# Gated linear attention and SoLU block on one core: third group's query transposes and scans exchanged, three small sums moved, and in two groups both state reads in one row

## The chip, the cores and the metric

One Trainium2 core. The metric is device time in microseconds (us) of the one core, the median of several runs. The profile is one profiled execution of the same program.

## The reference

An attention block with a decaying state, followed by a SoLU feed-forward block. Shapes: batch 4, 8 heads, 768 tokens, head size 48; 3072 tokens by 384 into 1024 hidden columns and back.

```python
for t in range(S):
    state = alpha[:, :, t, :, None] * state + einsum('bhd,bhe->bhde', k[:, :, t], v[:, :, t])
    y[:, :, t] = einsum('bhd,bhde->bhe', q[:, :, t], state)
x = y.transpose(0, 2, 1, 3).reshape(B * S, H * D)
h = x @ w_in
sm = exp(h - max(h)) / (sum(exp(h - max(h))) + 1e-9)
solu = h * sm
ln = (solu - mean(solu)) / sqrt(var(solu) + 1e-6) * g_ln
return ln @ w_out
```

## The kernel before, in words

The 768 tokens are cut into six groups of 128. A group holds 128 tokens of each of the four batches, so it has four chunks of 128 output rows. Each group goes through two parts, and the program is written so that the feed-forward of group g runs between the pieces of the attention of group g+1. Every engine works through its own queue in the order in which the program was written (the schedule is manual); engines wait for one another by semaphores. Nothing is reordered by a planner, so a step that is moved in the text is moved on every engine and DMA queue that it uses.

**Attention of group a**, in the order of the data:

- `load`, `load_v`: DMAs from SP's queue, into `an` (alpha), `kn`, `qn`, `vn`.
- `alpha_T`: alpha is transposed on VectorE (`firsts` L179 for 32 of a head's 48 columns, `lasts` L182 for the other 16) into `aT`; `scan_back` (L204) makes running products from the end, in three parts, into `hT`. `inverses` takes the reciprocal of the first column as the seed.
- `keys_T`, `keys`: keys are transposed on VectorE and multiplied by `hT` on GpSimd (L225).
- `scan_on(a, i)` (L204 too): the running products forward, in place in `aT`, for part i = 2 (the 16-column ends), 0 and 1 (heads 0 to 3 and 4 to 7).
- `lasts(qn, qe)`, `firsts(qn, qv)`: the queries are transposed on VectorE. `queries(i)` multiplies part i by `aT` on GpSimd (L253).
- `ends_of_decay` copies the group's whole decay into the last column of `qe` and `qv` (L240, L241). `move_lasts` and `move_firsts` are eight and four DMAs on SP's queue that lay queries and decay out in `q64` (printed as `lot` in the profile).
- `apart` writes two masked copies of `qe` beside `qv` on ScalarE (L245).
- `scores(a, half)`: 64 small matmuls on TensorE (L278), `masked(half)`: VectorE multiplies by the triangle (L289).
- `decay(a)`: GpSimd multiplies the state by the decay (L261). `read_state(half)`: 64 matmuls of the state with the moved queries (L333, tiles of 64 by 32); `read_values`: 128 matmuls of scores and values (L333, tiles of 128 by 32) into the same banks, then four copies on ScalarE into `x` (L363). `next_state`: the new keys and values are added to the state (L371, L381).

**Feed-forward of group g**: for each of eight column blocks s, `up(g, s)` is six matmuls of 512 columns (L394) into one of two `h` banks, exp on ScalarE (L408), h times exp on VectorE (L409, which frees the bank), a square on ScalarE (L412). `running` keeps two running sums over s, one on GpSimd and one on VectorE (both L427). `token_sums` (L454) turns these into sums by token: 32 matmuls, a transpose on VectorE (L467), and three small VectorE instructions (L469, L471, L473) whose result `d["s"]` only `finish` reads. `down(n, half)` is eight matmul steps (L507) for one chunk. `finish` scales a chunk (L532 to L548) and stores it.

The first group and most of the second are written out by hand (L699 to L843). From there a loop runs over g = 1 to 5 and s = 0 to 7. In it two tables, `first` for g = 1 and `usual` for the others, say which pieces of the attention of group g + 1 come ahead of `up` (head), behind it, after the running sums (middle), and after `down` (tail). So the attention of the third group, a = 2, lies in g = 1 by the table `first`, and that of the last two groups, a = 4 and a = 5, in g = 3 and g = 4 by `usual`. In `usual` the row at s = 6 has `read_state(0)` behind the running sums, then a `down`; s = 7 has `up`, `read_state(1)`, `read_values`.

In the third group the transposes of alpha and keys and the scans of parts 2 and 0 stand ahead of the loop (L842, L843):

```python
    scan_on(2, 2)
    scan_on(2, 0)
```

and in the loop the scan of part 1 stands at s = 1, the query transposes, their multiplications, the copies of the decay and the moves all at s = 2.

Of the kernel before, what the change touches and what calls it, by code (L numbers as in the profile page):

```python
# [9 lines left out]
FP = mybir.dt.float32  # L10
# [4 lines left out]
ALU = mybir.AluOpType  # L15
AX = mybir.AxisListType
P = 128
# [15 lines left out]
def fast_path(ctx, tc, q, k, v, alpha, moe_w_in, moe_w_out, moe_g_ln, out):  # L33
# [12 lines left out]
    nc = tc.nc  # L46
    B, H, S, D = q.shape
    NTOK, DM = out.shape
    DFF = moe_w_in.shape[1]
# [3 lines left out]
    NB = H + NP  # L53
# [8 lines left out]
    def pool(name, bufs, **kw):  # L62
        return ctx.enter_context(tc.tile_pool(name=name, bufs=bufs, **kw))
# [4 lines left out]
    small = pool("small", 4)  # L68
# [31 lines left out]
    qn = const.tile([P, H, TQ, D], FP, name="qn")  # L100
# [8 lines left out]
    SW = P + 1  # L109
# [7 lines left out]
    h4 = hT[:, 0 : NB * SW].rearrange("p (j s) -> p j s", s=SW)  # L117
# [3 lines left out]
    qv = const.tile([P, 2 * H, SW], FP, name="qv")  # L121
    qe = const.tile([P, NP, SW], FP, name="qe")
# [5 lines left out]
    gr = [dict() for _ in range(G)]  # L128
# [49 lines left out]
    def firsts(src, dst):  # L178
        nc.vector.transpose(out=dst.rearrange("p h (t u) -> p h u t", u=TQ), in_=src[:, :, :, 0:E0])  # L179

    def lasts(src, dst):
        nc.vector.transpose(  # L182
            out=dst.rearrange("p j (i t u) -> p u j i t", u=TQ, i=2),
            in_=src[:, :, :, E0:D].rearrange("p (j i) u d -> p u j i d", i=2),
        )
# [29 lines left out]
    def scan_on(g, i):  # L215
        part = slice(NP * i, NP * i + NP)
        scan(aT[:, part], aT[:, part], seed[:, part], False)
# [18 lines left out]
            i, c = divmod(b, 2)  # L236
            nc.sync.dma_start(out=q64[64 * i : 64 * i + E0, c], in_=qv[32 * b : 32 * b + 32, 0:H])

    def ends_of_decay():
        nc.gpsimd.tensor_copy(out=qe[:, :, P:SW], in_=h4[:, H:NB, 1:2])  # L240
        nc.gpsimd.tensor_copy(out=qv[:, 0:H, P:SW], in_=h4[:, 0:H, 1:2])  # L241

    def apart():
        for i in range(2):
# [41 lines left out]
    def masked(half, batches=range(B)):  # L286
        a = masks[half]
        for b in batches:
            nc.vector.tensor_tensor(  # L289
                out=sT[:, b, half * NP : half * NP + NP], in0=a[b], in1=mask[:, None, :].to_broadcast([P, NP, P]),  # L290
                op=ALU.mult,
            )
# [55 lines left out]
    def read_state(half):  # L348
        for four in range(8 * half, 8 * half + 8, 4):
            for c in range(2):  # L350
                for n, h, e in parts[four : four + 4]:
                    for i in range(2):
                        p = slice(64 * i, 64 * i + 64)
                        y_mm(2 * i + c, n, 64 * i, state[p, c, e(h)], q64[p, c, h, 0:P])
# [99 lines left out]
    def token_sums(g):  # L454


        d = gr[g]
        t = ps_a.tile([P, B, 2, 32], FP, tag="a3", name="rows") if g else ps_h.tile([P, B, 2, 32], FP, tag="h", name="rows")
        for b in range(B):
            for r in range(4):  # L460
                c = b * P + 32 * r
                nc.tensor.matmul(
                    t[quarter(r), b], lhsT=d["unit"][:, 0:32], rhs=d["p"][:, :, c : c + 32], start=True, stop=True,
                    tile_position=(0, 32 * r), skip_group_check=True,
                )
        tt = work.tile([P, B, 2, 32], FP, name="cols")
        nc.vector.transpose(out=tt.rearrange("p b i t -> p (b i t)"), in_=t.rearrange("p b i t -> p (b i t)"))  # L467
        s = sums[:, g * B : g * B + B]
        nc.vector.tensor_copy(out=s[:, :, 1:3], in_=tt[:, :, :, 0])  # L469
        sq = small.tile([P, B], FP, name="sq")  # L470
        nc.vector.tensor_tensor(out=sq, in0=s[:, :, 1], in1=s[:, :, 1], op=ALU.mult)  # L471
        d["s"] = small.tile([P, B], FP, name="s")
        nc.vector.scalar_tensor_tensor(  # L473
            out=d["s"], in0=sq, scalar=1e-6 * DFF, in1=s[:, :, 2], op0=ALU.mult, op1=ALU.add
        )

    def last_norm():

# [39 lines left out]
    def finish(n):  # L518
        g, b = divmod(n, B)
        d = st[n]  # L520
        s, whole = sums[:, n], d.get("held", d["o"])
        o = whole[:, 0:DM]
        t0 = b * S + g * P
        if g == G - 1:
            o_sb = work.tile([P, DM], FP, name="o_sb")
            r = gr[g]["r"][:, b : b + 1]
            nc.vector.tensor_scalar(out=o_sb[:, 0:P], in0=o[:, 0:P], scalar1=r, scalar2=None, op0=ALU.mult)  # L527
            nc.scalar.activation(out=o_sb[:, P:DM], in_=o[:, P:DM], func=AF.Copy, scale=r)  # L528
            nc.scalar.dma_start(out=out[t0 : t0 + P, :], in_=o_sb)
            d.clear()  # L530
            return
        nc.vector.tensor_copy(out=s[:, 0:1], in_=whole[:, DM : DM + 1])  # L532
        t = small.tile([P, 1], FP, name="t")
        nc.vector.scalar_tensor_tensor(
            out=t, in0=s[:, 0:1], scalar=-1.0 / DFF, in1=s[:, 0:1], op0=ALU.mult, op1=ALU.mult
        )
        nc.vector.tensor_tensor(out=s[:, 3:4], in0=t, in1=gr[g]["s"][:, b : b + 1], op=ALU.add)  # L537
        if g == 0:

            centred = work.tile([P, DM], FP, name="o_mean")  # L540
            nc.vector.scalar_tensor_tensor(
                out=centred, in0=mean_sb, scalar=s[:, 0:1], in1=o, op0=ALU.mult, op1=ALU.add
            )
            o = centred
        r = small.tile([P, 1], FP, name="r")
        nc.gpsimd.tensor_tensor(out=r, in0=s[:, 3:4], in1=mhalf, op=ALU.pow)  # L546
        o_sb = work.tile([P, DM], FP, name="o_sb")
        nc.scalar.activation(out=o_sb, in_=o, func=AF.Copy, scale=r)  # L548
        nc.sync.dma_start(out=out[t0 : t0 + P, :], in_=o_sb)
        d.clear()  # L550
# [166 lines left out]
    for i in (0, 2, 1):  # L717
        if i == 1:
# [3 lines left out]
            out=qe[:, :, 0:P] if i == 2 else qv[:, part, 0:P], in0=t[i], in1=aT[:, part, 1:SW], op=ALU.mult  # L722
# [98 lines left out]
    down(2, 1)  # L821
    scores(1, 1)
    masked(1)
    finish(0)
    finish(1)
    finish(2)
# [8 lines left out]
    for i in range(3):  # L835
# [3 lines left out]
    keys(2)  # L839
    load(k, kn, 3)  # L840
    down(3, 1, (2, 3))
    scan_on(2, 2)  # L842
    scan_on(2, 0)  # L843

    usual = dict(
        head={4: "keys_back", 5: "masked0", 6: "masked1"},
        behind={0: "v keys", 1: "on2 on0 on1", 2: "lasts firsts", 3: "apart", 5: "decay", 6: "alpha", 7: "back"},
        middle={6: "begin read0", 7: "read1 values"},  # L850
        tail={4: "scores0", 5: "scores1", 7: "kv"},
    )
    first = dict(
        head={3: "keys_back"},
        behind={
            0: "v", 1: "on1", 2: "lasts firsts", 3: "apart", 4: "scores0 masked0", 5: "scores1 masked1 decay",
            7: "alpha back",
        },
        tail={6: "begin read0"},
        middle={7: "read1 values over"},  # L860
    )

    def attend(a, what):

        more = a + 1 < G
        if what == "v":
            load_v(a)
        elif what == "keys":
            keys_T(a)
            keys(a)  # L870
            if more:
                load(k, kn, a + 1)
        elif what[:2] == "on":
            if what == "on2":
                inverses(a)
            scan_on(a, int(what[2]))
        elif what == "lasts":
            lasts(qn, qe[:, :, 0:P])
            ends_of_decay()
            queries(2)  # L880
            move_lasts()
        elif what == "firsts":
            firsts(qn, qv[:, 0:H, 0:P])
            queries(0)
            queries(1)
            move_firsts()
            if more:
                load(q, qn, a + 1)
        elif what == "apart":
            apart()  # L890
        elif what == "decay":
            decay(a)
        elif what == "keys_back":
            if more:
                keys_back(a)
        elif what[:6] == "scores":
            scores(a, int(what[6]))
        elif what[:6] == "masked":
            masked(int(what[6]))
        elif what == "alpha" and more:  # L900
            alpha_T(a + 1)
            if a > 2:
                attend(a, "over")
        elif what == "over" and more:
            alpha_over(a + 1)
            if a + 2 < G:
                load(alpha, an, a + 2)
        elif what == "back" and more:
            for i in range(3):
                scan_back(a + 1, i)  # L910
        elif what == "begin":
            read_begin()
        elif what[:4] == "read":
            read_state(int(what[4]))
        elif what == "values":
            read_values(a)
        elif what == "kv" and more and a != 4:
            next_state(a)
# [59 lines left out]
    def compare(out, x, bound, op):  # L978
# [6 lines left out]
        out=chunks[:, :, 2], in0=sums[:, :, 2], scalar=0.25, in1=sums[:, :, 3], op0=ALU.mult, op1=ALU.is_le  # L985
# [6 lines left out]
    else:  # L992
# [9 lines left out]
        out=bad, in0=all_ok[0:1, 0:1], scalar1=float(P * ends[-1]), scalar2=None, op0=ALU.is_lt  # L1002
# [451 lines left out]
```

## Time and profile before

| what | value |
|---|---|
| median of 3 runs | 368.37 us (367.83 to 369.05) |
| profiled execution, its time | 367.97 us |
| profiled execution, its span | 366.2 us |
| TensorE busy | 357.8 us (98% of the span) |
| VectorE busy | 245.0 us (67%) |
| ScalarE busy | 146.4 us (40%) |
| GpSimd busy | 132.2 us (36%) |
| DMA moved | 36.06 MB, mean 98 GB/s |
| TensorE clock granted | 1.0 throughout |

The span is from the first to the last instruction of the program; 1.8 us of the execution's time lie around it. Lines of the timeline give the start in us from the start of the span, the length, the engine, the line of the kernel, the operation, the tiles (output, arrow, inputs), the shape of the tile of the array for TensorE, the count, and in square brackets an idle stretch of the engine ahead of it with what ended it. Matmuls overlap in the pipe; so the distance between the starts of two neighbouring lines is what the first of them costs TensorE, not its length.

### The profile page before, as it was taken

The page shows a single profiled execution, that of the slowest core. Times are in us where ns is not written, and L with a number is a line of the kernel's source. Part 1 is how long each engine was busy: PE and PEld are TensorE (multiplying, and loading weights), DVE is VectorE, ACT ScalarE, POOL GpSimd, SP SyncE. Part 2 cuts the span into 40 slices and gives each one's busy share as a digit, 9 for nine tenths or more (in the row PEclk, how much of TensorE's full clock was granted, in tenths as well). Part 3 has the DMA queues.
Part 4 walks back from the last instruction along what each step waited for, and adds up shares of the span by engine and source line. Part 5 has one row for each costly group of instructions (what it writes and reads, how often), then busy time and mean ns, then how long its engine had stood idle before and what let it go on. Part 6 is the DMA issues. An engine that isn't in the chain of part 4 may idle for free. (4 is left out here: it accounts for less than half of the span.)

```text
span 366.2 us, 10036 instructions
## 1 busy us (share of the span) xinstructions
PE 357.8 (98%) x4341; PEld 215.0 (59%) x4341; DVE 245.0 (67%) x375; ACT 146.4 (40%) x260; POOL 132.2 (36%) x129
## 2 busy tenths in 40 slices
PE   8899999999999999999999999999999999999994
PEld 8784355666755566566575456475556565555552
DVE  0999989979998797936675935766946314345420
ACT  3647878182645262252521252431241132222110
POOL 7020000004449963774133764232773121233300
PEclk9999999999999999999999999999999999999999
DMA  9995995326196409463035354004041000000011
GB/s 180 183 338 152 204 309 124 88 67 159 50 234 141 109 21 180 85 152 94 21 92 112 83 121 126 3 25 88 21 107 55 0 25 0 24 21 22 23 47 51
DMA packets 72871, 36.06 MB, mean 98 GB/s; under 512 B 48232, under 2 KB 70000, under 8 KB 72816
## 3 DMA queue, kind: packets, MB, share of 16 engines
q1 hardware_dynamic: 71792, 34.39, 39.8%
q10 hardware_dynamic: 1024, 0.92, 0.8%
q8 instruction: 36, 0.59, 0.7%
q14 instruction: 19, 0.16, 0.2%
HBM read 25.30 MB, written 4.72 MB: 82 GB/s over the span
## 5 line engine op out<-in xcount | busy, mean ns | idle before, releaser
L507 PE MATMUL o<-w_out,room 128*128 128x385 f32 x384 | 134.0, 492 | 0.0
L394 PE MATMUL h<-x,w_in 128*128 128x512 f32 x288 | 131.7, 597 | 0.5 <-DVE g_col L642 0.5
L507 PEld LDWEIGHTS o<-w_out,room 128*128 128x128 f32 x384 | 71.0, 189 | 54.7 <-issue 13.1
L394 PEld LDWEIGHTS h<-x,w_in 128*128 128x128 f32 x288 | 53.2, 189 | 58.6 <-issue 48.5
L409 DVE TENSOR_TENSOR room<-h,e 128x512 f32<-128x512 f32 x40 | 27.5, 689 | 72.9 <-ACT e L408 72.9
L408 ACT ACTIVATE e<-h 128x512 f32<-128x512 f32 x40 | 24.0, 599 | 100.2 <-PE h L394 100.2
L427 POOL TENSOR_TENSOR p<-p,e 128x512 f32<-128x512 f32 x30 | 43.7, 1458 | 20.0 <-ACT e L408 19.9
L412 ACT ACTIVATE u<-room 128x512 f32<-128x512 f32 x40 | 25.2, 630 | 38.3 <-DVE room L409 38.3
L546 POOL TENSOR_TENSOR r<-sums,mhalf 128x1 f32<-128x1 f32 x20 | 14.8, 741 | 69.7 <-DVE sums L537 69.4
L289 DVE TENSOR_TENSOR sT<-a,mask 128x512 f32<-128x512 f32 x43 | 26.7, 681 | 8.0 <-PE a L278 7.9
L204 DVE TENSOR_TENSOR_SCAN hT<-aT,unit 128x516 f32<-128x516 f32 x18 | 24.4, 1399 | 7.6 <-ACT aT L703 7.5
L204 DVE TENSOR_TENSOR_SCAN aT<-aT,seed 128x516 f32<-128x516 f32 x18 | 27.4, 1551 | 0.2
L225 POOL TENSOR_TENSOR kT<-kT,hT 128x1024 f32<-128x1024 f32 (+1 forms) x8 | 14.2, 1800 | 32.7 <-DVE kT L179 32.7
L427 DVE TENSOR_TENSOR p<-p,u 128x512 f32<-128x512 f32 x30 | 22.5, 749 | 5.1 <-ACT u L412 5.1
L278 PEld LDWEIGHTS a<-qv,kT 32*128 32x128 f32 x704 | 21.4, 186 | 7.0 <-issue 2.6
L278 PE MATMUL a<-qv,kT 32*128 32x128 f32 x704 | 23.9, 278 | 0.4 <-POOL qv L253 0.3
L212 POOL COPY fend<-hT 128x12 f32<-128x12 f32 x6 | 3.1, 509 | 55.9 <-DVE hT L204 55.9
L333 PE MATMUL y<-sT,vn 128*32 128x128 f32 x768 | 22.6, 273 | 0.2 <-DVE sT L289 0.2
L333 PEld LDWEIGHTS y<-sT,vn 128*32 128x32 f32 x768 | 20.7, 110 | 1.6 <-issue 1.0
L196 ACT ACTIVATE sq<-an,mone 128x1536 uint8<-128x1536 f32 x12 | 18.9, 1572 | 0.2
L548 ACT ACTIVATE o_sb<-o,r 128x384 f32<-128x384 f32 x16 | 9.3, 582 | 18.5 <-POOL r L546 18.5
L261 POOL TENSOR_TENSOR state<-state,lot 128x384 f32<-128x384 f32 x10 | 8.8, 903 | 13.1 <-DMA lot<-qv 13.1
(148 smaller groups left out, 374.3 us busy)
## 6 DMA issues: line engine op xcount, KB each, us to landing
vn<-in_v_dram SPq DMA_DIRECT2D x24, 192.0 KB, 4.7
an<-in_alpha_dram SPq DMA_DIRECT2D x20, 192.0 KB, 4.1
out_dram<-o_sb SPq DMA_DIRECT2D x20, 192.0 KB, 1.9
room<-in_moe_w_out_dram SPq DMA_DIRECT2D x8, 384.0 KB, 5.5
kn<-in_k_dram SPq DMA_DIRECT2D x16, 192.0 KB, 5.6
qn<-in_q_dram SPq DMA_DIRECT2D x16, 192.0 KB, 4.1
lot<-qe SPq DMA_DIRECT2D x40, 64.5 KB, 2.1
lot<-qv SPq DMA_DIRECT2D x20, 129.0 KB, 2.4
```

Of the source, the lines that this page charges most:

```text
L196: nc.scalar.activation(out=sq, in_=x, func=AF.Relu, scale=sign, bias=mone, accum_out=over[:, g, i : i + 1])
L204: nc.vector.tensor_tensor_scan(out=o, data0=a, data1=s, initial=1.0, op0=ALU.mult, op1=ALU.add)
L278: nc.tensor.matmul(a[b][:, i], lhsT=kT[quarter(b), kb], rhs=qv[quarter(b), qb, 0:P], start=not last and not i, stop=bool(last), tile_posit ...
L289: nc.vector.tensor_tensor(out=sT[:, b, half * NP : half * NP + NP], in0=a[b], in1=mask[:, None, :].to_broadcast([P, NP, P]), op=ALU.mult,)
L333: nc.tensor.matmul(y_bank(b)[quarter(r), a], lhsT=lhsT, rhs=rhs, start=(b, r) not in begun, stop=stop, tile_position=(row, 32 * r), skip_g ...
L394: nc.tensor.matmul(h, lhsT=w_in[:, a, f * P : (f + 1) * P], rhs=d["x"][:, a].rearrange("p b t -> p (b t)"), start=(a == 0), stop=(a == KC ...
L408: nc.scalar.activation(out=e, in_=h, func=AF.Exp)
L409: nc.vector.tensor_tensor(out=u, in0=h, in1=e, op=ALU.mult)
L412: nc.scalar.activation(out=u2, in_=u, func=AF.Square)
L427: eng.tensor_tensor(out=p, in0=d[0][i] if f == 1 else p, in1=d[f][i], op=ALU.add)
L507: nc.tensor.matmul(d["o"][:, 0 : DM + 1], lhsT=u_of(g, f)[:, b * P : b * P + P], rhs=w_out[:, f], start=(f == 0), stop=(f == FC - 1), skip ...
L546: nc.gpsimd.tensor_tensor(out=r, in0=s[:, 3:4], in1=mhalf, op=ALU.pow)
```

## The change

It has three parts, which share no instruction.

1. **Third group (a = 2).** The transposes of the queries (`lasts` and `firsts`, both on VectorE) go ahead of the loop, in the place of the scans of parts 2 and 0. The scan of part 2 goes to s = 0, behind `up` and `load_v`. At s = 1 come the scan of part 0, the copies of the decay (now on ScalarE, not GpSimd), the multiplication of part 2 and the eight moves of `qe`. At s = 2 come the scan of part 1, the multiplications of parts 0 and 1, the four moves of `qv` and the load of the next queries.
2. **First group's sums by token.** The three small VectorE instructions at the end of `token_sums(0)` are put off from behind the transpose (some 25 us before `finish(0)`) to just ahead of `finish(0)`, behind `masked(1)`.
3. **Last two groups (a = 4, 5).** `read_state(0)` leaves s = 6 and stands at s = 7, just ahead of `read_state(1)` and `read_values`. For a = 2 and 3 it stays.

```diff
-    def ends_of_decay():
-        nc.gpsimd.tensor_copy(out=qe[:, :, P:SW], in_=h4[:, H:NB, 1:2])
-        nc.gpsimd.tensor_copy(out=qv[:, 0:H, P:SW], in_=h4[:, 0:H, 1:2])
+    def ends_of_decay(copy=nc.gpsimd.tensor_copy):
+        copy(out=qe[:, :, P:SW], in_=h4[:, H:NB, 1:2])
+        copy(out=qv[:, 0:H, P:SW], in_=h4[:, 0:H, 1:2])
...
         s = sums[:, g * B : g * B + B]
-        nc.vector.tensor_copy(out=s[:, :, 1:3], in_=tt[:, :, :, 0])
-        sq = small.tile([P, B], FP, name="sq")
...
+        def rest():
+            nc.vector.tensor_copy(out=s[:, :, 1:3], in_=tt[:, :, :, 0])
+            sq = small.tile([P, B], FP, name="sq")
...
+        if g:
+            rest()
+        else:
+            d["rest"] = rest
...
     masked(1)
+    gr[0]["rest"]()
     finish(0)
...
     down(3, 1, (2, 3))
-    scan_on(2, 2)
-    scan_on(2, 0)
+    lasts(qn, qe[:, :, 0:P])
+    firsts(qn, qv[:, 0:H, 0:P])
...
     usual = dict(
...
-        middle={6: "begin read0", 7: "read1 values"},
+        middle={6: "begin", 7: "read1 values"},
...
     first = dict(
...
-            0: "v", 1: "on1", 2: "lasts firsts", 3: "apart", 4: "scores0 masked0", 5: "scores1 masked1 decay",
+            0: "v on2", 1: "on0 lasts", 2: "on1 firsts", 3: "apart", 4: "scores0 masked0", 5: "scores1 masked1 decay",
...
-        tail={6: "begin read0"},
+        tail={6: "begin"},
...
-            if what == "on2":
+            if what == "on2" and a > 2:
                 inverses(a)
             scan_on(a, int(what[2]))
         elif what == "lasts":
-            lasts(qn, qe[:, :, 0:P])
-            ends_of_decay()
+            if a > 2:
+                lasts(qn, qe[:, :, 0:P])
+            ends_of_decay(nc.gpsimd.tensor_copy if a > 2 else nc.scalar.copy)
             queries(2)
             move_lasts()
         elif what == "firsts":
-            firsts(qn, qv[:, 0:H, 0:P])
+            if a > 2:
+                firsts(qn, qv[:, 0:H, 0:P])
             queries(0)
             queries(1)
...
         elif what == "begin":
             read_begin()
-        elif what[:4] == "read":
-            read_state(int(what[4]))
+            if a < 4:
+                read_state(0)
+        elif what == "read1":
+            if a > 3:
+                read_state(0)
+            read_state(1)
```

More of the change, by code (lines that the diff above doesn't have):

```diff
@@ L468, in token_sums @@
         s = sums[:, g * B : g * B + B]
-        nc.vector.tensor_copy(out=s[:, :, 1:3], in_=tt[:, :, :, 0])
-        sq = small.tile([P, B], FP, name="sq")
[L471 to L475, printed above, removed]
+        def rest():
+            nc.vector.tensor_copy(out=s[:, :, 1:3], in_=tt[:, :, :, 0])
+            sq = small.tile([P, B], FP, name="sq")
+            nc.vector.tensor_tensor(out=sq, in0=s[:, :, 1], in1=s[:, :, 1], op=ALU.mult)
+            d["s"] = small.tile([P, B], FP, name="s")
+            nc.vector.scalar_tensor_tensor(
+                out=d["s"], in0=sq, scalar=1e-6 * DFF, in1=s[:, :, 2], op0=ALU.mult, op1=ALU.add
+            )
+        if g:
+            rest()
+        else:
+            d["rest"] = rest
     def last_norm():
```

## Prediction

> **What bounds the kernel now.** I read the page's busy row first, then TensorE's timeline from end to end, then the waits of its weight loads.
>
> ```profile
> PE 357.8 (98%) x4341; PEld 215.0 (59%) x4341; DVE 245.0 (67%) x375; ACT 146.4 (40%) x260; POOL 132.2 (36%) x129
> PE   8899999999999999999999999999999999999994
> ```
>
> TensorE has work in hand nearly always, but matmul ends are modelled, so a busy TensorE may still be late. I therefore take the distance between starts. In the sixth group, where its attention lies in the loop's g = 4, the timeline has:
>
> ```profile
> 263.09 2.74 PE L394 MATMUL h<-x,w_in 128*128 128x512 f32 x6
> 265.66 2.76 PE L507 MATMUL o<-w_out,room 128*128 128x385 f32 x8
> 268.25 2.74 PE L394 MATMUL h<-x,w_in 128*128 128x512 f32 x6
> ...
> 280.88 2.07 PE L278 MATMUL a<-qv,kT 32*128 32x128 f32 x64
> 282.87 2.84 PE L394 MATMUL h<-x,w_in 128*128 128x512 f32 x6
> 285.64 1.16 PE L333 MATMUL y<-lot,state 64*32 64x128 f32 x64
> 286.74 2.86 PE L507 MATMUL o<-w_out,room 128*128 128x385 f32 x8
> 289.44 2.74 PE L394 MATMUL h<-x,w_in 128*128 128x512 f32 x6
> 292.10 1.16 PE L333 MATMUL y<-lot,state 64*32 64x128 f32 x64
> 293.19 3.70 PE L333 MATMUL y<-sT,vn 128*32 128x128 f32 x128
> ```
>
> Between whole-array neighbours an `h` row costs 2.57 us (265.66 - 263.09) and an `o` row 2.59. Next to a row of small tiles each pays 0.09 to 0.11 us a side: `h` after scores and before the state 2.77, `o` after the state 2.70, `h` before the state 2.66. From 131 to 361 us I find these same distances row for row: TensorE never waits there, and time falls only if its own rows get cheaper. Before that I find stops at three scores rows; the views show what ended the first two:
>
> ```profile
> 77.87 2.69 PE L278 MATMUL a<-qv,kT 32*128 32x128 f32 x64
> 113.12 2.26 PE L278 MATMUL a<-qv,kT 32*128 32x128 f32 x64 [0.26 <-POOL qv L253]
> PEld a L278 <- DVE qv L811: 0.3, 1, 0.3
> ```
>
> A scores row costs 2.00 when nothing is late. The second group's first one goes on to 80.49, 2.62: **0.62 late**, until VectorE's L811 (77.76, 0.69) ends. The third group's first one starts 0.32 late (12 `h` matmuls take 5.57, not 5.25), until `queries(0)` on GpSimd is done at 113.08, and takes 2.19: another 0.19, until `apart` on ScalarE ends at 114.62. **0.51 late** in all. Its second one, 2.14, waits 0.14 for a bank that `masked(0)` frees.
>
> **What the Trainium skill says.** TensorEngine Tiling (Array Packing), Key Properties: changing the tiling mode drains TensorE. The trace agrees: those 0.09 to 0.11 us a side. SBUF — State Buffer, "SBUF: two separate sides": VectorE, with two SBUF inputs, and GpSimd take a shared port pair as an exclusive lock for a whole instruction; the other blocks. The trace agrees: a scan takes 1.23 alone (the median of all), and the two at 97.56, beside GpSimd's key multiplication, 4.69 together, the longer of them 2.61; `ends_of_decay`'s copy takes 0.20 alone (72.00) and 1.13 beside a scan (106.34). A transpose has one input, and is not held: 1.11 and 2.05 beside GpSimd.
>
> ```profile
> 97.56 4.69 DVE L204 TENSOR_TENSOR_SCAN aT<-aT,seed 128x516 f32<-128x516 f32 x2
> 105.68 1.79 DVE L204 TENSOR_TENSOR_SCAN aT<-aT,seed 128x516 f32<-128x516 f32 x1
> 108.59 1.11 DVE L182 STREAM_TRANSPOSE qe<-qn 128x512 f32<-128x512 f32 x1
> 109.55 2.05 DVE L179 STREAM_TRANSPOSE qv<-qn 128x1024 f32<-128x1024 f32 x1
> 112.02 0.69 DVE L409 TENSOR_TENSOR room<-h,e 128x512 f32<-128x512 f32 x1
> ```
>
> **First sums later.** The three instructions start at 63.16, 63.37 and 63.57 and the next starts at 63.65; without them it would start as the transpose before them ends, 63.13. That is 0.52 to 0.58, I take 0.55. VectorE is then busy without a gap to L811, so L811 ends at 77.90, and the scores' stop shrinks from 0.62 to 0.07: **gain 0.55**. `apart`, the other input, ended at 77.37, and comes forward with its scan. The 0.55 comes back on VectorE after `masked(1)`: VectorE stood idle 1.97 us ahead of `masked(0)`, and with scores 0.55 earlier that idle shrinks by as much, so `finish(0)` starts at 88.0 to 88.1 as now. Behind `rest` wait only the finishes (GpSimd's power, ScalarE's outputs at 89.51 to 92.8) and the scans from 90.95; the copies of `x` at 92.95 are 0.1 us behind the last output, so the first `up`, now at 96.83, can be 0.55 earlier too. If that cover were gone, `up` would lose what is gained, no more.
>
> **Third group.** VectorE does the same instructions in another order; I walk its queue on today's clock. Keys' transposes end at 97.56. `lasts` and `firsts` cost 0.97 and 1.9 from start to start: 100.4 (today the two scans last to 102.2, held by the key multiplications; those now run unhindered, done near 100.3 instead of 101.2). L409 for s = 0: 101.0. `finish(3)`, 1.0: 102.0. Two state sums, 1.0: 103.0. Scan 2 at 1.23: 104.2. L409 for s = 1: 104.8. Scan 0, held 0.5 by `queries(2)` (1.09, from 104.2): 106.5. Running sum: 107.1. L409 for s = 2: 107.7. Scan 1, held 0.7 by GpSimd's running sum: 109.6. Running sum, held 1.1 by `queries(0)`: 111.3. L409 for s = 3: 111.9, against 112.7 today. So `queries(0)` is done near 110.7 instead of 113.08, and `apart` near 113.8 instead of 114.62. TensorE, 0.55 early and not stopped, reaches these scores at 112.25; the half that needs `apart` begins at 113.25, first with its even heads (first ScalarE instruction, near 113.15), then odd ones at 113.75. They end near 114.3 instead of 115.32: 0.55 is kept and **0.51 more gained**. The 0.14 of the second scores I leave.
>
> The other queues: GpSimd loses 1.85 us of copies (1.13 + 0.72). ScalarE gets two copies of 4 and 8 elements; no such row exists, the nearest is its accumulator read, 0.19. Two of those, 0.4 near 105.9, lie between a square and the exp of s = 2, whose VectorE partner is due only at 107.1: nothing, or up to 0.4 if that exp sets L409. SP sends `vn` (five us, behind `finish(3)`'s store, from 105.05), then the eight moves of `qe` (5.17), the four of `qv` (3.81), the queries' load. `qe` is ready near 106, so the moves follow `vn` at once, at 110.0 or earlier instead of 110.90, and `decay` (121.42 now) gains 0.9 to 1.8. TensorE reads the state at 123.00, 0.73 after the state's first half is released, so 1.06 us earlier still fits.
>
> **Both reads in one row.** With `h` and `o` side by side at s = 6, `h` loses its side (2.77 to the 2.68 of the `h` row at 275.51) and `o` its side (2.70 to 2.59). In the read row itself, matmuls come in eights every 0.109 us, the first gap is 0.14 and the last matmul is followed after 0.199; one row of 128 has these ends once: 2.06 instead of 2.18. 0.09 + 0.11 + 0.12 = 0.32 a group, **0.64 for two**. The bounds are 0.2 (the two sides) and 0.4 a group. `x` is copied at the same distance from the next `up`, with an `o` row between.
>
> **Sum.** 0.55 + 0.51 + 0.64 = 1.70. From the profiled execution, 367.97 (span 366.2 and 1.8 around it), that gives 366.27. This execution is 0.40 under the median of 368.37, so on the median's scale 366.67; I say **366.7**. A measurement of this kernel can tell about 0.3%, 1.1 us, from no change: 367.27 is the line.
>
> **Rivals.**
>
> - *The stop only moves* (0.20). TensorE comes 0.55 early, but `apart` stays tied to L409 of s = 3 and ends at 114.6 as now; both early gains are then waited away at the same place, and 0.64 is left: 367.7, within 0.3%. For it: `apart` is in ScalarE's queue behind that chain, and my walk has it only 0.8 earlier. Against: VectorE had 4.7 us of scans held by GpSimd that are now transposes, which are not held.
> - *The lock decides* (0.13), slower. In the loop each scan stands beside a GpSimd instruction. At the longest price for all three scans, 2.61 against 1.23, 1.73 and 1.9 in my walk, VectorE loses 1.4 + 0.9 + 0.7 = 3.0, and a running sum at 1.50 (today's worst) 0.7 more: L409 of s = 3 ends at 115.6, `apart` at 117.5, the scores near 118.2 instead of 115.32. 2.9 lost, 0.64 gained: 370.6. It turns slower by 0.3% once that L409 ends past 114.45, 2.5 us after my walk. For it: `scan aT` takes 2.2 in each later group. Against: that is one in three, the others take 1.21 to 1.23.
> - *The row of reads saves nothing beyond its sides* (0.05): gain 1.46, 366.9; if not even those, 1.06, 367.3 and on the line. The tiling page says that drains come with a mode change, and the modes are the same in the row, which speaks against the latter.
>
> **How the numbers follow.** The forecast gets 0.62. Its ends: 1.2 (the drop to 0.2 a group, 0.3 of the third group's stop left) and 2.3 (0.4 a group, the 0.14 and leftover 0.07 too, the later 0.05 of a state read), so 366.1 to 367.2. Adding the stop that moves and the foot of the slower case, I give 365.9 to 368.5. Faster 0.66, within 0.3% 0.21, slower 0.13.
>
> **What would show it.** Right: the second group's first scores row costs 2.05 to 2.1; the third group's 2.0 to 2.1 with no wait for GpSimd; L409 of s = 3 ends near 111 on the new clock; in g = 3 and 4 one state row of 128 at about 2.06 with `h` and `o` at 2.6 to 2.7 ahead. Wrong: scans above 2 us one after another between 102 and 110; `apart` ending at the same distance after the key transposes as now; or a new idle stretch of TensorE past 131 us.

## The result and the profile after

| | before | changed |
|---|---|---|
| median of 12 runs | 368.49 us (367.83 to 369.05) | 367.47 us (366.66 to 368.38) |
| ratio of the runs | | 0.997, 95% interval 0.996 to 0.998 |
| profiled execution, span | 366.2 us | 366.6 us |
| TensorE busy | 357.8 us | 358.0 us |

The changed kernel is 1.02 us faster (0.28%), where 1.7 was forecast. The time lies inside the stated range, beyond the likeliest case's own range, and just short of the line that divides "faster" from "within 0.3%".

The profiled execution of the changed kernel is, at 368.38, the slowest of its twelve, and its span is longer than that of before. This is why spans are not compared here. The stretch ahead of the first state matmul (`kv`, L371) is the same program in both and took 32.31 instead of 31.13 us. Most of this comes from one wait in the first group's values, which cost 5.86 us instead of 4.23 (0.6 of it is made good before `kv`, where TensorE waits less for VectorE):

```profile
23.09 0.64 PE L333 MATMUL y<-sT,vn 128*32 128x128 f32 x14 [0.20 <-DVE sT L289]
25.15 3.04 PE L333 MATMUL y<-sT,vn 128*32 128x128 f32 x102 [1.41 <-issue]
```

Behind 26 of the 128 matmuls TensorE stands for 1.41 us, and "issue" says that it waited for nothing which the profile shows: no semaphore, no DMA of the program. The experiments come back to this wait. All sums below are therefore counted from that matmul, to the lone small matmul `all_ok` near the end (L999, or L1012 in the changed kernel): 322.04 us before, 321.05 after, **0.99 less**. That this is so close to the 1.02 of the medians is partly luck: a second profile of the kernel before, taken later (`before_again`), has 322.75 there, so the difference of two single profiles is uncertain by some 0.7. Subtract 1.18 from a time after to set it beside one before.

The timeline of TensorE after, in the second group, then the third, then where the fifth group's reads lie. The line numbers behind the small sums are six higher: `down` is L513.

```profile
79.06 2.07 PE L278 MATMUL a<-qv,kT 32*128 32x128 f32 x64
81.05 2.86 PE L513 MATMUL o<-w_out,room 128*128 128x385 f32 x8
...
92.33 3.92 PE L333 MATMUL y<-sT,vn 128*32 128x128 f32 x128
96.18 1.24 PE L513 MATMUL o<-w_out,room 128*128 128x385 f32 x3
...
113.56 2.43 PE L278 MATMUL a<-qv,kT 32*128 32x128 f32 x64
115.92 2.84 PE L394 MATMUL h<-x,w_in 128*128 128x512 f32 x6
...
123.60 1.35 PE L333 MATMUL y<-lot,state 64*32 64x128 f32 x64
124.88 2.84 PE L394 MATMUL h<-x,w_in 128*128 128x512 f32 x6
...
234.82 2.74 PE L394 MATMUL h<-x,w_in 128*128 128x512 f32 x6
237.49 2.04 PE L333 MATMUL y<-lot,state 64*32 64x128 f32 x128
239.46 3.70 PE L333 MATMUL y<-sT,vn 128*32 128x128 f32 x128
```

Read the distances between starts again. The second group's first scores cost 1.99 (81.05 - 79.06), with no stop. Its values cost 3.85, where 3.63 was the price in every group but the first. The third group's first scores begin without a wait but cost 2.36, and its state row costs 1.28 instead of 1.09. The merged read row costs 1.97. Row by row, in us:

| row | before | after | difference |
|---|---|---|---|
| second group, first scores | 2.62 | 2.00 | -0.62 |
| second group, values | 3.63 | 3.85 | +0.22 |
| third group, wait ahead of the first scores | 0.32 | 0.00 | -0.32 |
| third group, first scores | 2.19 | 2.36 | +0.17 |
| third group, first state row | 1.09 | 1.28 | +0.19 |
| fifth and sixth group, reads with their neighbours | | | -0.41 each |
| sixth group, values | 3.63 | 3.87 | +0.24 |

The sum is -0.94; the 0.05 to the measured 0.99 is spread over other rows. The two long values rows, +0.46 together, turn out below to be waits for instructions, and their length differs from profile to profile.

Two lines of waits of TensorE's weight loads in the changed kernel (us in total, times, longest) tell which waits those are:

```profile
PEld y L333 <- issue: 7.6, 13, 1.7
PEld a L278 <- ACT qv L245: 0.4, 1, 0.4
```

The second is `apart` (L245), for the third group's scores. In the first, the waits without a releaser, mode changes stand too; the longest was 0.8 before, and the 1.7 is the one just shown.

### The profile page after: what moved, and what is told of

Same layout as the page of the kernel before. It is cut to its first block, busy times and chain, and to the rows that moved or that the text cites. A ratio compares the mean times of both kernels' runs of the same rounds, so it can differ in the third digit from the quotient of the medians.

```text
span 366.6 us, 10041 instructions
## 1 busy us (share of the span) xinstructions
PE 358.0 (98%) x4341; PEld 216.0 (59%) x4341; DVE 243.9 (67%) x375; ACT 146.5 (40%) x262; POOL 130.3 (36%) x127
## 5 line engine op out<-in xcount | busy, mean ns | idle before, releaser
L513 PE MATMUL o<-w_out,room 128*128 128x385 f32 x384 | 133.8, 491 | 0.0
L513 PEld LDWEIGHTS o<-w_out,room 128*128 128x128 f32 x384 | 71.1, 189 | 55.2 <-issue 13.4
L409 DVE TENSOR_TENSOR room<-h,e 128x512 f32<-128x512 f32 x40 | 27.6, 690 | 72.7 <-ACT e L408 72.7
L427 POOL TENSOR_TENSOR p<-p,e 128x512 f32<-128x512 f32 x30 | 43.1, 1437 | 20.3 <-ACT e L408 20.2
L204 DVE TENSOR_TENSOR_SCAN aT<-aT,seed 128x516 f32<-128x516 f32 x18 | 25.4, 1441 | 0.2
L225 POOL TENSOR_TENSOR kT<-kT,hT 128x1024 f32<-128x1024 f32 (+1 forms) x8 | 13.3, 1687 | 33.6 <-DVE kT L179 33.6
L427 DVE TENSOR_TENSOR p<-p,u 128x512 f32<-128x512 f32 x30 | 21.7, 723 | 5.1 <-ACT u L412 5.1
L278 PE MATMUL a<-qv,kT 32*128 32x128 f32 x704 | 23.7, 279 | 0.2 <-ACT qv L245 0.2
```

What stands on the lines that cost most here:

```text
L204: nc.vector.tensor_tensor_scan(out=o, data0=a, data1=s, initial=1.0, op0=ALU.mult, op1=ALU.add)
L278: nc.tensor.matmul(a[b][:, i], lhsT=kT[quarter(b), kb], rhs=qv[quarter(b), qb, 0:P], start=not last and not i, stop=bool(last), tile_posit ...
L409: nc.vector.tensor_tensor(out=u, in0=h, in1=e, op=ALU.mult)
L427: eng.tensor_tensor(out=p, in0=d[0][i] if f == 1 else p, in1=d[f][i], op=ALU.add)
L513: nc.tensor.matmul(d["o"][:, 0 : DM + 1], lhsT=u_of(g, f)[:, b * P : b * P + P], rhs=w_out[:, f], start=(f == 0), stop=(f == FC - 1), skip ...
```

## The experiments

Two explanations stood against each other at first. **A**: parts 1 and 2 draw on the same stop, at `apart`, so they are worth little alone and something together. **B**: part 1 costs by itself, through the locked scans or late moves. Later a third question came up: what the "issue" waits are.

### Each part alone, and two of three

The edits are those of the change, one part at a time.

**Part 1 alone** (`p1_third_group`). 

> The kernel before with the first part alone (third group's transposes ahead of its scans, decay copies on ScalarE). Theory A (parts 1 and 2 draw on the same stop, at apart): TensorE is not early here, so it reaches the third group's first scores at today's 112.8 and apart, near 114.0, is no longer late: 0.4 to 0.5 us faster than before, first scores row 2.0 to 2.1. Theory B (part 1 costs by itself, through the locked scans or the late moves): no gain or a loss of up to 0.2 us, the row stays at 2.2 or more.

Measured: 368.30 against 368.33 before, ratio 0.9998 (0.9988 to 1.0009). In its profile the third group's scores stand without any stop. TensorE's timeline:

```profile
112.95 2.07 PE L278 MATMUL a<-qv,kT 32*128 32x128 f32 x64
114.95 2.84 PE L394 MATMUL h<-x,w_in 128*128 128x512 f32 x6
```

The rows agree with A: 2.00 from start to start, and `kv` to the end of the third group's values takes 99.86 instead of 100.46. The medians agree with B's "no gain". That profile was of the fastest of its 14 runs. Its second group's values took 3.86, though the program up to there is that of before. Why the median doesn't show the 0.5 us of the rows stays open; the wait in the first group's values, 1.1 us or more in some executions and absent in this profile, is one candidate.

**Part 2 alone** (`p2_first_sums`). 

> The kernel before with the second part alone (first group's three small instructions later). Both theories: the second group's first scores row falls from 2.62 to 2.00. Theory A: that 0.62 is then waited away at the third group's first scores, where apart has not moved: total gain 0 to 0.15 us. Theory B: 0.4 to 0.6 us stay.

Measured: 368.74, ratio 1.0009 (0.9997 to 1.0021): 0.4 us slower, not clear of zero. The scores row did fall, to 2.06. But the gain was gone before the third group, in a place that neither theory had named. TensorE's timeline:

```profile
91.58 3.70 PE L333 MATMUL y<-sT,vn 128*32 128x128 f32 x126
95.47 0.38 PE L333 MATMUL y<-sT,vn 128*32 128x128 f32 x2 [0.19 <-issue]
```

The last two of 128 matmuls come 0.46 us after the one ahead of them; the row costs 4.20 instead of 3.63. It ends 64.26 us after the first `kv`, where the kernel before, which came to the row 0.6 later, ends it at 64.29.

**Part 3 alone** (`p3_reads`). 

> The kernel before with the third part alone (both state reads in one row in the last two groups). By the row distances of the changed kernel: 0.41 us for each group, 0.8 us in all, less up to 0.25 for each values row whose instruction fetch comes late. If the fetch is worse because of the new order, the long values row shows again in the sixth group; if it was chance, it does not.

Measured: 367.66, ratio 0.9976 (0.9967 to 0.9985), 0.67 us faster. Both read rows cost 1.97 and both values rows behind them 3.63. The sixth group's values cost 3.63 in three more profiles with this order of TensorE's work too (`p23_without_third`, `xf_stores_later`, `x12_apart_v`). So merging alone does not make that row long. The second group's values are long here as well (3.86), though nothing ahead of them was changed.

**Parts 2 and 3** (`p23_without_third`). 

> The changed kernel without its first part. Theory A (the stop only moves): 0.62 from the second part is lost again at the third group, 0.8 stay: 0.7 to 1.0 us faster than before, about 0.3 slower than the changed kernel. Theory B (part 1 gives nothing): as fast as the changed kernel, about 1.0 us faster than before.

Measured: 368.03, ratio 0.9987 (0.9979 to 0.9996), 0.30 us faster, less than either theory expected. The second group's values cost 4.19, and the third group's scores are reached 81.99 us after `kv`, exactly as before the change.

**Parts 1 and 2** (`p12_without_reads`). 

> The changed kernel without its third part (reads split as before). If the third part is independent of the others, the row stays as in the changed kernel up to 223 us and 0.8 us are missing after: 0.2 to 0.5 us faster than before. Parts 1 and 2 alone gave about 0 and a loss of 0.4; if they simply added, this kernel would be 0.4 slower than before.

Measured: 367.88 against 368.41, ratio 0.9986 (0.9979 to 0.9994), 0.53 us faster. Apart, the two parts gave 0 and -0.4, neither clear of zero; together they gave 0.5. Part 3 is worth 0.67 alone and, as a difference, 0.5 on top of the others.

That parts 1 and 2 do more together than apart is what A says, but the rows do not show A's reason. `apart` ends 83.48 us after `kv` before, 83.46 with part 2 alone, 82.78 with part 1 alone and 82.87 with both. In the profile with both, of the slowest of its 21 runs, TensorE however reaches these scores at 81.64, no earlier than before (81.67): a values row of 4.23 ahead of them had eaten what part 2 gave. From `kv` to `all_ok` that profile is 0.34 shorter than before, and the one of part 1 alone 0.56. So the 0.5 us of parts 1 and 2 together is shown by the runs; how they share it is not.

### The two remaining stops of the third group

The changed kernel's ScalarE timeline shows where `apart` stands, and SP's timeline where the moves (`lot<-qe`) stand:

```profile
106.53 0.18 ACT L240 COPY qe<-hT 128x4 f32<-128x4 f32 x1
...
109.95 0.63 ACT L412 ACTIVATE u<-room 128x512 f32<-128x512 f32 x1 [2.15 <-DVE room L409]
...
113.34 0.63 ACT L412 ACTIVATE u<-room 128x512 f32<-128x512 f32 x1 [0.76 <-DVE room L409]
113.88 1.32 ACT L245 ACTIVATE qv<-qe,parity 128x512 f32<-128x512 f32 x2
```

```profile
105.16 6.61 SPq L176 DMA_DIRECT2D vn<-in_v_dram  x4
111.88 5.25 SPq L232 DMA_DIRECT2D lot<-qe  x8
```

In VectorE's timeline L409 of s = 3, which the last square ahead of `apart` waits for, has itself waited for ScalarE:

```profile
112.62 0.69 DVE L409 TENSOR_TENSOR room<-h,e 128x512 f32<-128x512 f32 x1 [0.68 <-ACT e L408]
```

The experiment `x12_apart_v` moves both `apart` and the loads. `qe` is ready on GpSimd at 106.61, but `apart` stands behind nine ScalarE instructions (part of them shown) and is reached at 113.88. And SP needs 6.61 us to issue the four loads of `vn` that took it 4.97 before; 3.10 of them go to a single issue, where most take 0.4 to 0.6. Twelve loads of 192 KB stand ahead of the moves, alpha's, the keys' and `vn`'s own; the reading, which no view shows directly, is that SP is held until earlier ones have landed.

```diff
-    0: "v on2", 1: "on0 lasts", 2: "on1 firsts", 3: "apart", ...
+    0: "on2", 1: "on0 lasts apart", 2: "on1 firsts v", ...
```

> The changed kernel with apart moved from s = 3 to s = 1, behind the moves of qe, and the third group's load_v from s = 0 to behind the moves of qv. If apart is late by its place in ScalarE's queue, behind the key copies and the exp of s = 3, the third group's first scores row falls from 2.36 to 2.00; if the scans and their lock hold it, it stays above 2.2. If SP's queue is held by the loads' drain, the moves leave near 107 instead of 111.9 and the state row falls from 1.28 to 1.09; if not, it stays. Both right: 0.3 to 0.6 us faster than the changed kernel. A load_v later by five us must still land before the values at 128.7; if it does not, the values row is late and it gets slower.

Measured: 366.56 against 368.06 before, ratio 0.9956 (0.9944 to 0.9968), 1.5 us faster than before. TensorE's and SP's timelines:

```profile
113.70 2.07 PE L278 MATMUL a<-qv,kT 32*128 32x128 f32 x64
115.70 2.84 PE L394 MATMUL h<-x,w_in 128*128 128x512 f32 x6
...
123.24 1.17 PE L333 MATMUL y<-lot,state 64*32 64x128 f32 x64
124.33 2.84 PE L394 MATMUL h<-x,w_in 128*128 128x512 f32 x6
```

```profile
106.95 5.28 SPq L232 DMA_DIRECT2D lot<-qe  x8
...
117.81 5.58 SPq L176 DMA_DIRECT2D vn<-in_v_dram  x4
```

Both scores cost 2.00, the state row 1.09, the moves leave 4.4 us earlier counted from `kv` (75.15 instead of 79.57), and the later `vn` holds nothing up. This profile alone would not settle the scores, because TensorE comes to them 0.65 later than in the changed kernel (81.90 us after `kv`, not 81.25). The experiments `x12s_16_fewer` and `x12r_16_back` below have the same edit; in both profiles TensorE comes at 81.04, earlier than in the changed kernel, and the rows still cost 2.00 and 1.09 or 1.10. TensorE's timeline in `x12s_16_fewer`:

```profile
112.63 2.07 PE L278 MATMUL a<-qv,kT 32*128 32x128 f32 x64
114.63 2.84 PE L394 MATMUL h<-x,w_in 128*128 128x512 f32 x6
```

So the place in ScalarE's queue held the scores, and the loads ahead in SP's queue held the state row. B's lock is not what decides: the running sum beside GpSimd still takes 1.70 here (DVE, L427). The median of this kernel is the lowest of all versions, but against the changed kernel it is 0.9956 to 0.997, with intervals that overlap, so a lead over the changed kernel is not shown.

### What the "issue" waits are

A gap that no semaphore ends can come from TensorE's supply of instructions. The first form of this theory, F, says that the stores of `finish(0)` to `finish(2)`, which run at the time of the second group's values, slow the fetch; its rival G ties the row's length to something else. To tell them apart, the stores are put behind the values:

```diff
     masked(1)
     gr[0]["rest"]()
-    finish(0)
-    finish(1)
-    finish(2)
...
     load(alpha, an, 3)
+    finish(0)
+    finish(1)
+    finish(2)
```

**On part 2 alone** (`p2f_sums_stores_later`). 

> The kernel before with the second part, and finish(0) to finish(2), with their three stores, put behind the second group's values and the load of the next alpha. Theory F (with part 2 alone the early 0.6 us is eaten in the second group's values row, whose last matmuls wait for an instruction fetch slowed by the three stores): the fetch near 92 us takes under 1.1 us, the values row 3.6 to 3.7 instead of 4.20, and its end moves from 64.3 to about 63.7 after the first state matmul; the third group then takes 0.3 of this back: 0.3 to 0.6 us faster than part 2 alone. Theory G (the row's length is tied to something else, such as the start of the row against the fetch's own fixed pace): the row stays at 4.0 or more, no faster than part 2 alone.

**On the changed kernel** (`xf_stores_later`). 

> The changed kernel with finish(0) to finish(2) and their stores behind the second group's values and the load of the next alpha. Theory F: values row 3.63 instead of 3.85, 0.2 us come through to the third group's scores, where apart stands in the way: 0 to 0.2 us faster than the changed kernel. Theory G: values row 3.85 or longer, no difference.

Measured: 377.55 (ratio 1.0262) and 375.72 (1.0207), far slower (9.5 and 7.7 us), for a reason that neither theory had. VectorE's timeline of the second:

```profile
99.54 0.61 DVE L547 SCALAR_TENSOR_TENSOR o_mean<-mean_sb,sums,o 128x384 f32<-128x384 f32 x1 [8.95 <-ACT o_sb L554]
```

The third chunk's `o_mean` needs one of two buffers back. ScalarE reads them, and it now has the copies of `x` and two long sweeps of alpha first, so VectorE stands for 8.95 us; all of the third group's scans stand behind it.

As for the row: 3.63 in the first, 3.96 in the second. In the second, nothing but one queue moved any data on this core from 88 to 96 us, the stretch around the row:

```profile
q8 instruction: 2, 0.03, 1.7%
```

So this wait needs neither a store nor any other load beside it.

**Everything together** (`xall`): the moved `apart` and `load_v`, the moved stores, and both reads in one row in the third and fourth group too.

```diff
         elif what == "begin":
             read_begin()
-            if a < 4:
-                read_state(0)
         elif what == "read1":
-            if a > 3:
-                read_state(0)
+            read_state(0)
             read_state(1)
```

> The changed kernel with all of these: apart at s = 1, load_v behind the moves, finish(0) to finish(2) behind the values, and both state reads in one row in the third and fourth group too. From the row distances: 0.36 and 0.19 in the third group, 0.2 in the second group's values, 0.4 for the fourth group's reads and 0.4 for the third's: 1.2 to 1.6 us faster than the changed kernel, 366.0 or so. If merged rows make instruction fetches late, single values rows of 3.9 to 4.2 take part of it back.

Measured: 376.68 (1.0228), through the same wait of VectorE (8.69 us), where 366.0 or so was expected. But its merged rows show the issue waits at their largest. TensorE's timeline in the third group:

```profile
133.26 2.04 PE L333 MATMUL y<-lot,state 64*32 64x128 f32 x128
135.23 1.94 PE L333 MATMUL y<-sT,vn 128*32 128x128 f32 x58
137.56 2.17 PE L333 MATMUL y<-sT,vn 128*32 128x128 f32 x70 [0.38 <-issue]
139.65 0.59 PE L513 MATMUL o<-w_out,room 128*128 128x385 f32 x1
```

The values row costs 4.42 here and 5.15 in the fourth group: merging saves 0.4 and pays 0.8 and 1.5.

Now count TensorE's instructions (weight loads, matmuls and the sequencer's) in order of time from 0, and take the number of the first one behind a gap without a releaser. In the second group's values of the changed kernel it is 3009, in the sixth group's 8129, in the first group's 961; in part 2 alone 3009; in the kernel with everything together 4033 and 5313. Divided by 256, every one of these leaves 193: the gaps stand at the same place of a block of 256 instructions. The page's table of DMA queues shows what has that size:

```profile
q8 instruction: 36, 0.59, 0.7%
```

36 transfers of 0.59 MB in all are 16.4 KB each, 64 bytes for each of 256 instructions, and TensorE's 8740 instructions fill 34 such blocks. That queue 8 carries them is inferred from these numbers. A values row holds 256 instructions and uses them up in 3.6 us, a merged read row in 1.97; an `h` row of 2.57 us uses only 12. But the gap is not bound to rows of small tiles: in the profile of `x12_apart_v` it stands in the first `h` row behind `kv`, which had used up 256 instructions in 1.5 us, again at place 193 of a block. TensorE's timeline:

```profile
33.30 2.41 PE L394 MATMUL h<-x,w_in 128*128 128x512 f32 x5
36.23 8.31 PE L394 MATMUL h<-x,w_in 128*128 128x512 f32 x19 [0.52 <-issue]
```

In the six kernels with the change or some of its parts where the second group's values were long, from 3.85 to 4.23, the gap ended 1.4 to 1.5 us after the packets of a queue 8 transfer had ended, the transfer itself taking 1.04 to 1.74 us. In the kernel before, the row came to that place 1.65 us after the packets, and there was no gap.

This can be asked of every block. Pair the transfers in order with the instructions 449, 705, 961 and so on, which stand at place 193 of a block. In the fourteen profiles of this case that makes 462 pairs. In none of them does that instruction run less than 1.19 us after the packets of its transfer ended, and in all the long rows named here it runs 1.19 to 1.52 us after. So what makes a row long is that its transfer ends late for it. The first group's values fit too: their transfer ended at 21.8 to 22.1 us in the profiles where they cost 4.23, and at 22.9 to 23.7 where they cost 5.27 to 5.86.

To test the place in the stream by itself, `x12s_16_fewer` takes 16 instructions out of the kernel of `x12_apart_v` ahead of it, the four warm-up matmuls at 13 us. Theory F now says that the gaps are tied to places of the stream, its rival H that they are contention of the moment:

```diff
-    warm(4, ps_a, "a1")
```

> The kernel of x12_apart_v without the four warm-up matmuls at 13 us: 16 instructions of TensorE's stream fewer ahead of everything that follows, no other change. Theory F (TensorE's instructions come in blocks of 256, all issue gaps stand at index 193 or 194 of such a block, and a row of small tiles that uses a block up in under some 3.6 us waits for the next one): all later block ends move 16 instructions on. In the second group's values row the block end leaves the row: 3.63 instead of 3.81. In the fifth group's read row (start 236.96 in x12_apart_v, now 10 instructions behind a block end) the block end falls at instruction 6, so 256 instructions of 7.7 ns follow in one block: the values row behind it starts with a wait of 1.3 to 1.8 us. In all 1.0 to 1.6 us slower than x12_apart_v, about 367.8. Theory H (the gaps are contention of the moment with stores and loads, not places in the stream): rows as in x12_apart_v, same time within 0.3.

Measured: 367.11 against 368.41, ratio 0.9966 (0.9954 to 0.9978). The second group's values are at 3.63, as theory F has it:

```profile
91.62 3.70 PE L333 MATMUL y<-sT,vn 128*32 128x128 f32 x128
95.25 1.56 PE L513 MATMUL o<-w_out,room 128*128 128x385 f32 x4
```

That alone proves little, since four other profiles have 3.63 with all instructions in place. The first group's values say more. Their gap is at 961 as in `x12_apart_v`, though the row begins some 16 instructions earlier in the stream: it keeps its place in the stream, not in the row. The row costs 4.44 and in the next experiment 4.27, where `x12_apart_v` had 5.56.

The wait expected in the fifth group did not come, though: 1.97 and 3.63. Its block had been transferred early, 5.9 us before it was needed. How far ahead the instructions are fetched is therefore not as theory F had it: with the pairing above, a transfer began from 8 to 301 instructions ahead of its block. And the time, 0.1% above that of `x12_apart_v` and not 1.0 to 1.6 us, agrees with H rather than with F.

**16 put back** (`x12r_16_back`), in `token_sums`:

```diff
-        for b in range(B):
+        for b in (0, *range(B)) if g == 1 else range(B):
             for r in range(4):
```

> The kernel of x12s_16_fewer with 16 instructions put back behind the second group's values: the first four matmuls of the sums by token of g = 1 are done twice (cost about 0.14 us of row). Theory F: the second group's values row stays at 3.63, the fifth group's rows are back at 1.97 and 3.63 without a wait: 0 to 0.3 us faster than x12_apart_v, 1.0 to 1.6 faster than x12s_16_fewer. Theory H: no difference between the three beyond 0.3.

Measured: 366.90, ratio 0.9961 (0.9947 to 0.9974). Second group's values 3.63 again; the fifth group's rows as expected; in the sixth group a values row of 4.14, with its gap at place 193 of a block. The ratios of the three kernels, 0.9956, 0.9966 and 0.9961, lie within one another's intervals, so the place of the blocks has no effect on the time that these runs could show.

**The kernel before once more** (`before_again`), with no edit. 

> The kernel before, unchanged, profiled once more. If the block ends of TensorE's instructions cost it as well, the second group's values row, which starts 2 instructions behind a block end as in all kernels, takes 3.8 to 4.2 here and not the 3.63 of the first profile: the profile that the prediction was made from was a lucky one by 0.2 to 0.6 us. If the row is 3.63 again, the row is long only where the small sums were moved or TensorE comes early. The first scores row of the second group should again be 2.2 to 2.6, that of the third group start 0.3 late and take 2.2.

Measured: one run, 368.94. The values row is 3.63 again. But in `p1_third_group` and `p3_reads`, whose program up to that row is the one of before, it took 3.86; so its length is a matter of the execution, and the +0.22 in the table above can't be charged to the change. The first group's values are 4.23 in both profiles of the kernel before; of ten profiles of kernels with some of the change and all their instructions, three have 4.23 and seven 5.27 to 5.86. The second group's first scores took 3.01, later still than 2.62.

## Why the prediction was right or wrong

- **TensorE's own rows set the time: right.** From 133 us on the rows after have the distances of before, save the merged ones with their neighbours and one values row.
- **First sums later, 0.55: right in its place, then lost downstream.** The row gave 0.62. The step that failed is the one that gave its cover, "`up` can be 0.55 earlier too": ScalarE was ready to copy `x`, but the values row that it copies came late. Its end is 0.42 earlier than before in the changed kernel's profile, and 0.03 earlier with part 2 alone. A values row was taken at 3.63 whatever came ahead; the term missing from the sum is the supply of instructions, 0.22 here and 0.24 in the sixth group. What part 2 is worth in the runs is not settled: beside nothing and beside part 3 it cost 0.4, beside part 1 it gave 0.5.
- **Third group, 0.51 more: wrong in size.** `apart` was to end 0.8 earlier and ended 0.59 earlier. In VectorE's walk the running sum of s = 1 was priced at 0.6; it took 1.69 beside GpSimd's. What follows it was cheaper than in the walk, so VectorE had made this good by the running sum of s = 2. But L409 of s = 2 had come 1.0 late, with it ScalarE's square, the key copies and the exp of s = 3, and L409 of s = 3 had to wait 0.68 for that exp. The walk followed VectorE's queue and left out this stretch of ScalarE's. TensorE came 0.42 early instead of 0.55, and row and wait together gave 0.15 instead of 0.51. That is the rival of the stop that only moves, in part.
- **The moves: wrong.** "At 110.0 or earlier" took SP's five us for `vn` as a fixed price of issuing. It was 6.61 here and 5.58 in `x12_apart_v`, with a single issue of over 3 us in each. The moves left at 111.88 (110.70 on the clock of before), 0.2 earlier than before instead of 0.9 to 1.8, and TensorE, 0.58 early, waited 0.19 for the decay.
- **Both reads in one row, 0.64: right, a little low.** It gave 0.41 a group: the row is 1.97, not 2.06, and the `h` and `o` beside it lost their sides as said.
- **The lock decides: not so.** Scans of 1.22, 1.82 and 1.52 stood where 2.61 each was feared.

So, in the rows of two profiles, the three numbers of the sum were 0.62, -0.04 and 0.82, less 0.46 of issue waits, against 0.55, 0.51 and 0.64. The runs bear out the third alone by itself. That the time still lies in the stated range is owed to the range's width, which was there for the rivals: the 1.02 is nearer to the 0.64 of the first rival than to 1.70. The chance of "within 0.3%" (0.21) was too small beside that of "faster" (0.66): the effect sits on the line.

What stays open: why part 1 alone shows 0.5 us in its rows and nothing in its median, and how parts 1 and 2 share their gain; what sets the moment at which a transfer of instructions begins, and so makes the wait in the first group's values come in some executions and not in others; and whether stores or loads make such a transfer longer.

## What to carry to other kernels

When one engine is never idle, read the distances between the starts of its rows; a row that is longer than its equals, with a gap that has no releaser, is a stop like any other. Where two instructions hold a stop together, look up who is second, and where it stands in its engine's queue, before you price the first: here the third group's 0.51 gave 0.15 until `apart` had moved too. And look at DMA issues that take longer than their like: the moves behind one of 3.10 us left 4.4 us earlier once they were put ahead of the loads. A gain of half a microsecond in the rows of one profile is not yet a gain in the median: part 1 alone is the example.

## What the runs showed of the hardware that was not expected

- By all that the traces show, TensorE's instructions arrive in transfers of 16.4 KB, and every gap without a releaser that was looked at here stands at the end of a block of 256 instructions. In 462 pairs no block began less than 1.19 us after its transfer's packets ended. A row of small tiles, 7.7 to 14 ns an instruction, can run into the next block's arrival: 0.2 to 1.7 us a time; a mode change costs 0.1.
- Merging two rows of small tiles saved 0.41 us in each of two groups, and cost 0.4 and 1.1 net in two others of one profile, where a block end inside the values behind it was waited for.
- Copies of 4 and 8 elements on ScalarE take 0.18 and 0.20 us; the same on GpSimd took 1.13 and 0.72 beside VectorE's work.
